# Attention with sinks, then a mixture of attention experts: eight rings of work buffers become two shared pools, with a new instruction list

## The chip, the core and the metric

The kernel runs on one core of one Trainium2 chip. The metric is the device time of one execution in microseconds (us); before the change it is 373.31 us, the median of 3 runs (372.42 to 373.54). A core has a matrix engine (PE, with its weight loads PEld), a vector engine (DVE), a scalar engine (ACT), a general engine (POOL) and a sync engine (SP) that issues the transfers. Each works through its own list of instructions in order and waits for the others through semaphores.

## What is computed

For 4 batches, 8 heads, 768 positions and a head size of 64, the first stage is attention in which each position sees the first 4 positions (the sinks) and the 128 latest ones. Its output, 768 x 512 for each batch, goes through 4 expert attentions, causal and with full rows, each with its own projections; each position keeps 2 of the 4 by a gate.

```python
scores = scale * np.matmul(q, k.transpose(0, 1, 3, 2))
keep = is_sink | in_window
a = softmax(np.where(keep, scores, -1e9))
x = np.matmul(a, v)                      # per head, heads side by side
logits = x @ w_gate                      # top 2 of 4 experts, softmax weights w
for e in range(4):
    q, k, v = x @ wq[e], x @ wk[e], x @ wv[e]
    a = softmax(causal(scale * q @ k.T))
    out += w_e * (a @ v @ wo[e])         # where e is among the two
```

## The kernel before

The work is cut into units: for each batch 4 units of two heads of the first stage (`first`, banded rows) and 2 units of two experts of the second (`second`, wide rows of 1 to 6 blocks of 128 keys). A row of 128 queries goes through the same chain everywhere. PE makes the scores (L664 and L677 for the band, L669 for wide rows) into PSUM banks `b`; DVE masks them, takes the minimum and writes the probabilities' buffer `p` or, for 5 or 6 blocks, `pw` (L919, L955, L842); ACT takes the exponential there with its sum (L924, L959, L854); DVE makes the factor (L718, L719); POOL, or ACT, scales (L933, L980, L864, L862); PE transposes 64 x 64 pieces (L730) into two banks; ACT and DVE copy these to the transposed buffer `pt` (L551, L553, L780); PE multiplies with the values (L703, L707 for the sinks). ACT and DVE split a finished batch chunk `x` into two parts (L534, L539), and the projections (L1055 for queries and keys, L1082 for values) follow, and at the end of a batch the output product (L1131), whose rows go out through a buffer `o`.

The matmuls use the array in four shapes, which the profile writes as rows*columns: 128*128 (projections and output), 64*128 (scores and transposes), 128*64 (products with the values) and 64*64 (L677, an alternative form of a band's score step with 4 matmuls of 196 columns in place of 2 of 260).

The order of all work is a list, `ORDER`, written out in the program: one number for each step, with a letter that puts a step on ACT (a), DVE (v) or POOL (p) or takes the 64*64 form (q). The steps are emitted in that order. The buffer that a step writes is chosen at that moment by `slot`: of the ring with the step's tag the one that a table of costs says comes free first. The real waits are the semaphores that follow from it. While the planned time is under 130 us, `fill_in` puts matmuls on a zero tile (`nought`, L365 to L369) into gaps of the plan on PE. They compute nothing that is used.

```python
best = (None, None)
for n, b in enumerate(self.held[tag]):
    if n in taken:
        continue
    t = 0.0 if b is None else b.free_at(e)
    if t is not None and (best[0] is None or t < best[0]):
        best = (t, n)
return best
```

Before the change each kind of data has a ring of its own: 3 buffers for loaded q (`qn`), 2 for k (`kn`), 3 for v (`vn`), 2 for turned k (`kx`), 12 `p`, 4 `pw`, 4 `pt`, 2 for the differences of v (`dv`) and 2 output rows (`o`).

Of the kernel before, what the change touches and what calls it, by code (L numbers as in the profile page):

```python
# [39 lines left out]
0 44 39 45 46 47 49 1 56 34 42 40 58v 50a 48 51a 57v 52 53v 54a 64 65 67 43 41 37 55 75 76 59 61a 38 60v 66 86q 78 2 87 90 79  # L40
63 114 88 91 77 80 92 81 143 93 97 121q 122 35 98 94 142 68 3 125 95 99 115 69 89 116 123 238 126 96 118 124 70 100 117 119
101 127 239 82 120 83a 148 149v 150v 155 156v 157a 144 71 145 151 84v 72a 73a 128 152 146v 147a 160 153v 171 154v 161 4 163
189 172 162 164 173 102 174 193 182 210q 175 183 186 184 241 187 194 185 190 211 191 243a 242a 217 103 176 244 221 214 218
212 188 195 335 192 129 130 219 245a 5 222 177 246a 251 104a 165 215 247 6 105 220 166 108 252a 267 268 270 253a 256 216 106a
109a 269 430 196 248 131 249a 250a 159 271 107a 257 334 213 259 133 136 25 36 258 134a 197 278q 279 285q 62 158 282 280 283
281 306 289 74 307 286 308 287 223 290 224 111 132a 135a 284 198 313q 291 310 431 137v 311 260 312 225 272 288 314 226 340
199 273 201 433 110 317 200a 292 293 315 203a 138 205a 202a 318 341v 204 261 342a 85 139 112 337 343 316 140 338a 167 113
339a 168a 254 436 319 141 309 344 363 347 169a 240 320 346a 374q 364 366 345a 349a 227 375 378 348a 381q 32 262 26 376 228a
379 229 28 178 294 380 231a 321 33 385 179a 233a 382 230a 386 180a 365 383 384 170 207 30 518 434 232 387 322 29 263 295 402q
234 264v 265v 352 206 377 297 300 296a 403 301a 353 355 404 406 388 298a 181 235 274 299a 407 437 409 208 323 367 275a 209  # L50
276a 356 410 368 411 324a 27 354 435 490 413 255 336 405 408 266 494 303 412 414 325 277 491 31 415 389 350 326a 328 327a 357
451 329a 302 390 492 495 416 236 452 369 358 417 454 418 391 304 237 392v 370 371a 395a 372a 393 330 331 397a 359 394a 360a
351 361a 419 16 21 17 305 396 462q 420v 23 22 423v 453 421 422a 469q 463 473 519 464 19 362 373 399 424 332 466 467 470 425a
522 18 398 440 1086 400 524 465 455 496 24 20 426 427 523 855 401 658 659 441 443 525 428 521 550q 429 471 474 456 468 475
551 557q 552 553 497q 498 499 438 554 660 646 501 472 476 661 444 457 477 442 561 7 562 558 559 555 662 333 478 647 648 560
528 8 9 663 10 502 539 14 15 479 529 531 540 542 766 578q 585q 652 481 11 503 586 563 649 769 480a 12 13 579 767 580 582 587
432 484 583 482a 589 653 532 584 654 655 770 650 651 606 636 543 445 439 446 854 526 590 1092 493 858 530 500 504 505 533 520
534 612 485a 607 618 773 588 857 608 656 541 657 1089 613 637 624 527 619 630 609 631 611 506 625 620 544 632 610a 861 638
614 581 639 633 640a 483v 615 635 626 768 621 627 617 634a 447 556 696 616a 623 641 629 859 642 643 591 592 628a 697 448a 709
507 449a 622a 545 699 458 459a 460a 564 710 711 712 664 665 666 667 508v 509 513a 450 698 644 511v 461 487 514 593 594 700  # L60
510a 512 771 645 670 683 701 668 702 486 669 671 862 724 713 488 672 704p 684 685 703a 686 725 489 535 536a 537a 515 516 546
787 726 517 565 788 727 790 729 547a 728 674 548a 566 687 744 745 791 747 673 746 688 705 748 714 772 567 689 730 675 1175
789 749 569 568v 570v 573v 690p 731 942 750 751 706a 707a 752 572 943 792 948 949 944 950 945 571v 951 952 676 691p 953 538
549 595 946 860 947 574 677a 1087 775 776 678p 777 596a 599v 679 575 680a 597 681a 732 682 779 598a 708 600 576 601a 715 717p
716p 692 718 780 577 693a 719a 778 602 694v 798q 805q 793 753 720v 802 799 826q 806 809 603 721 800 810 827 828 733 807 755a
604 605 803 695 734p 864 829 781 830 875 831 808 804 865 866 833q 867 754p 876 921q 914q 811 735p 878 1090 837 868 915 722
918 916 919 877 834 723 879 954 955 956 801 838 812 835 869 1422 1093 832 925 920 922 917 926 960 839 923 813 957 961 962 958
814 963 959 836 964 736 965 737a 738a 880 870 840 924 760 761a 762a 992 993 994 756 757a 758a 1005 815 740 739 1006 1007 816a
741a 817 820 821v 841 759 742a 1008 782 1176 783 819v 842 784v 818a 927 979 1091 980 785a 843 856 995 928 774 881 893q 886q
981 897 743 887 890 1009 888 996 844a 894 847a 929 863 786 823 889 891 892 898 895 899 845 763 849v 848 871 846a 872v 930 896  # L70
794 873a 900 822 795a 1020 796a 901 902 1010 997 966 967 968 998 982 850 983 764 797 1021 824 851 882 1022 883a 765 825 884a
903 905 909a 906a 931 933 932v 970 1146q 874 908 852 999p 984 934a 1011 1012p 904a 907a 936 853 1013p 985 935v 885 969 1147
# [242 lines left out]
def kernel(  # L315
# [14 lines left out]
    nc = tc.nc  # L330
# [912 lines left out]
```

## Time and profile before

| | |
|---|---|
| median of 3 runs | 373.31 us |
| the profiled execution | 374.27 us, of which the span from the first to the last instruction is 372.2 us |
| PE busy | 364.9 us, 98% of the span |
| PEld, DVE, ACT, POOL busy | 85%, 82%, 76%, 55% |
| granted PE clock | 1.00 of 2.4 GHz |
| moved by DMA | 28.42 MB, mean 76 GB/s |

Busy time is what the records of an engine cover. Records of one engine can overlap: the next instruction starts before the one before it has ended. So the pace of a kind of work is read from one start to the next, and a matmul's own duration is longer than its share. The ends of matmuls are modelled, so a busy PE can still stand for some tens of nanoseconds between two matmuls.

### The profile page before, as it was taken

The page shows a single profiled execution, that of the slowest core. Times are in us where ns is not written, and L with a number is a line of the kernel's source. Part 1 is how long each engine was busy: PE and PEld are TensorE (multiplying, and loading weights), DVE is VectorE, ACT ScalarE, POOL GpSimd, SP SyncE. Part 2 cuts the span into 40 slices and gives each one's busy share as a digit, 9 for nine tenths or more (in the row PEclk, how much of TensorE's full clock was granted, in tenths as well). Part 3 has the DMA queues.
Part 4 walks back from the last instruction along what each step waited for, and adds up shares of the span by engine and source line. Part 5 has one row for each costly group of instructions (what it writes and reads, how often), then busy time and mean ns, then how long its engine had stood idle before and what let it go on. Part 6 is the DMA issues. An engine that isn't in the chain of part 4 may idle for free.

```text
span 372.2 us, 12873 instructions
## 1 busy us (share of the span) xinstructions
PE 364.9 (98%) x4588; PEld 315.7 (85%) x4588; DVE 305.6 (82%) x1415; ACT 284.2 (76%) x984; POOL 203.6 (55%) x395
## 2 busy tenths in 40 slices
PE   8999999999999999999999999999999999999995
PEld 7667878998888888988798889978889889988884
DVE  5899999899999988889989798797879748277851
ACT  3899987798899886468878797589877783539841
POOL 6699966769477184182945185374546260066510
PEclk9999999999999999999999999999999999999999
DMA  8999689900453073046407042013000000011113
GB/s 188 207 168 190 139 148 171 169 4 3 89 104 68 2 145 85 1 136 100 96 4 130 1 71 60 31 59 101 30 4 3 2 2 3 0 53 64 58 53 118
DMA packets 124175, 28.42 MB, mean 76 GB/s; under 512 B 120592, under 2 KB 120848, under 8 KB 124112
## 3 DMA queue, kind: packets, MB, share of 16 engines
q1 hardware_dynamic: 123568, 27.48, 35.6%
q8 instruction: 36, 0.59, 0.7%
q14 instruction: 27, 0.22, 0.2%
q10 hardware_dynamic: 544, 0.13, 0.2%
HBM read 21.05 MB, written 6.29 MB: 73 GB/s over the span
## 4 chain that ended last, share of the span: by engine, by line
PE 88%; DVE 3%; POOL 3%; DMA 2%; issue 2%; ACT 1%; SPq 0%; ACTq 0%; POOLq 0%; DVEq 0%
PE b L703 19%; PE b L1055 18%; PE b L730 11%; PE b L1082 10%; PE b L669 9%; PE b L1131 9%; PE b L664 5%; PE b L677 5%; POOL pw L864 2%; PE b L707 1%; PE b L369 1%; DMA qn<-in_q_dram 1%; POOL p L864 1%; DMA v<-in_moe_wk_dram 1%; ACT p L854 1%
## 5 line engine op out<-in xcount | busy, mean ns | idle before, releaser
L551 ACT ACTIVATE pt<-b 128x256 f32<-128x256 f32 (+3 forms) x186 | 66.8, 407 | 12.7 <-PE b L730 10.3
L959 ACT ACTIVATE p<-p,st 128x132 f32<-128x132 f32 x128 | 51.2, 406 | 6.3 <-DVE st L955 6.1
L933 POOL TENSOR_TENSOR p<-p,st 128x520 f32<-128x520 f32 (+1 forms) x32 | 26.7, 833 | 31.8 <-DVE st L719 22.7
L669 PE MATMUL b<-ks,qs 64*128 64x384 f32 (+3 forms) x384 | 42.1, 339 | 0.0
L703 PE MATMUL b<-pt,v 128*64 128x128 f32 x672 | 41.5, 275 | 0.0
L730 PE MATMUL b<-ident,p 64*128 64x64 f32 x768 | 40.4, 228 | 0.0
L730 PEld LDWEIGHTS b<-ident,p 64*128 64x128 f32 x768 | 33.8, 139 | 6.1 <-issue 1.9
L703 PEld LDWEIGHTS b<-pt,v 128*64 128x64 f32 x672 | 36.5, 137 | 2.5 <-issue 0.7
L703 PE MATMUL b<-pt,vn 128*64 128x128 f32 x448 | 38.0, 279 | 0.0
L1082 PE MATMUL b<-wvh,x 128*128 128x260 f32 x192 | 37.6, 285 | 0.0
L854 ACT ACTIVATE p<-p,st 128x384 f32<-128x384 f32 (+3 forms) x64 | 35.7, 560 | 2.1 <-DVE st L842 1.9
L952 DVE COPY_PREDICATED b<-earlier,b 128x128 f32<-128x128 int32 x128 | 33.6, 288 | 2.8 <-PE b L677 2.3
L955 DVE CUSTOM_DVE_ANT_0 p<-b,pair_mask 128x132 f32<-128x132 f32 x128 | 34.1, 289 | 1.1
L1131 PE MATMUL b<-woh,y 128*128 128x512 f32 (+1 forms) x100 | 34.8, 392 | 0.0
L669 PEld LDWEIGHTS b<-ks,qs 64*128 64x128 f32 x384 | 31.4, 186 | 2.6 <-issue 0.9
L980 POOL TENSOR_TENSOR p<-p,st 128x512 f32<-128x512 f32 x32 | 33.2, 1040 | 0.0
L1055 PE MATMUL b<-x,wqh 128*128 128x512 f32 (+1 forms) x128 | 33.2, 345 | 0.0
L722 POOL TENSOR_TENSOR st<-st,gate 128x2 f32<-128x2 f32 x48 | 9.1, 195 | 44.0 <-DVE st L719 39.5
L1055 PE MATMUL b<-x,wkh 128*128 128x512 f32 (+1 forms) x128 | 33.0, 343 | 0.0
L854 ACT ACTIVATE pw<-pw,st 128x640 f32<-128x640 f32 (+1 forms) x32 | 28.1, 879 | 5.6 <-DVE st L842 5.6
L1082 PEld LDWEIGHTS b<-wvh,x 128*128 128x128 f32 x192 | 30.7, 188 | 0.7
L864 POOL TENSOR_TENSOR pw<-pw,st 128x640 f32<-128x640 f32 (+1 forms) x23 | 30.8, 1356 | 0.9
(137 smaller groups left out, 1049.5 us busy)
## 6 DMA issues: line engine op xcount, KB each, us to landing
vn<-in_v_dram SPq DMA_DIRECT2D x32, 192.0 KB, 3.7
out_dram<-o SPq DMA_DIRECT2D x23, 256.0 KB, 2.0
qn<-in_q_dram SPq DMA_DIRECT2D x48, 96.0 KB, 2.6
kn<-in_k_dram SPq DMA_DIRECT2D x48, 96.0 KB, 2.7
kn<-in_k_dram SPq DMA_DIRECT2D x6, 192.0 KB, 3.6
qn<-in_q_dram SPq DMA_DIRECT2D x6, 192.0 KB, 4.8
o<-in_moe_wo_dram SPq DMA_DIRECT2D x2, 256.0 KB, 3.3
v<-in_moe_wk_dram SPq DMA_DIRECT2D x4, 128.0 KB, 3.1
```

Of the source, the lines that this page charges most:

```text
L551: nc.scalar.activation(dst(), src(), AF.Copy)
L669: nc.tensor.matmul(o, self.qs.t[hs, a, qs], self.ks.t[hs, b, ks], start=n == 0, stop=n == 2)
L703: nc.tensor.matmul(o[e * 64:e * 64 + 64], lhs, rhs, start=e not in self.begun, stop=last and self.done == len(self.steps))
L730: nc.tensor.transpose(t[g].t[:, n, :], x[gs], ident[gs, gs])
L854: nc.scalar.activation(x, x, AF.Exp, bias=st.t[:, 0, es], scale=-1.0, accum_out=st.t[:, 1, es])
L864: nc.gpsimd.tensor_mul(x, x, st.t[:, 2, e:e + 1].to_broadcast([128, n * 128]))
L952: nc.vector.copy_predicated(s2[e].t[:, :128], earlier.bitcast(I32), s2[e].t[:, SW:RW])
L955: nc.vector.tensor_tensor_reduce(out=p.t[:, n, :], in0=s2[e].t[:, :SW], in1=pair_mask, scale=-scale, scalar=BIG, op0=OP.add, op1=OP.min, a ...
L959: nc.scalar.activation(p.t[:, n, :], p.t[:, n, :], AF.Exp, bias=st.t[:, 0, n:n + 1], scale=-1.0, accum_out=st.t[:, 1, n:n + 1])
L1055: nc.tensor.matmul(t.t, w[a][:, c, es], X[b, c].t[:, x, cs], start=c == 0 and m == 0, stop=c == NCH - 1 and m == 2)
L1082: nc.tensor.matmul(t.t[:, :VW], X[b, c].t[:, a, qs], W["wv"][w][:, c, :], start=c == 0 and n == 0, stop=c == NCH - 1 and n == 2)
L1131: nc.tensor.matmul(t.t[:, a0:z0], Y[b, c].t[:, a, qs], W["wo"][w][:, c, a0:z0], start=c == 0 and n == 0, stop=c == EP - 1 and n == 2)
```

## The change

The eight rings `qn`, `kn`, `vn`, `kx`, `pw`, `pt`, `dv`, `o` and the ring `p` become two pools: 15 buffers `n` of 792 columns and 22 buffers `p` of 528. A loaded q, k or v, a turned k, a row of 5 or 6 blocks and a transposed piece of 6 sub-blocks take any free `n`; other probabilities, shorter transposed pieces, differences, the loaded output weights and the output rows take any free `p`. A band's transposed piece, formerly one `pt` of 8 sub-blocks, is now two `p` of 4. A wide row with 4 blocks has its transposes in two parts of 2 blocks, which adds 32 steps (2707 to 2739). One mask is stored in 128 columns less its unused part. The list `ORDER` is new in full, also its letters. Of the list one line of each stands for the rest.

```diff
-0 44 39 45 46 47 49 1 56 34 42 40 58v 50a 48 51a 57v 52 53v 54a 64 65 67 43 41 37 55 75 76 59 61a 38 60v 66 86q 78 2 87 90 79
...
+44 39 45 0 46 1 49 50a 51a 52 54v 53v 64 65 56 47 34 48 40 2 143 59 55 75 57a 67 58v 61v 60a 37 86 35 76 68 114 38 78 41 66
...
@@ -348,10 +349,10 @@
-    kinds = {"qn": (3, 768, F32), "kn": (2, 768, F32), "vn": (3, 768, F32), "qs": (1, 2 * S, F32R), "ks": (1, 2 * NB * SW, F32R),
-             "x": (6, 2 * S, F32R), "kx": (2, NB * SW, F32), "v2": (1, 1536, F32), "y0": (1, 2 * S, F32R), "y1": (1, 2 * S, F32R), "p": (12, 4 * SW, F32), "pw": (4, 768, F32),
-             "dv": (2, 512, F32), "pt": (4, 1024, F32), "psk": (4, 128, F32), "sk": (2, 128, F32R), "vs": (2, 4 * D, F32R),
-             "o": (2, 512, F32), "gate": (2, 4 * NB * E, F32), "gates": (1, 2 * NB * E * E, F32), "st": (6, 20, F32),
+    kinds = {"n": (15, NB * SW, F32), "p": (22, 4 * SW, F32), "qs": (1, 2 * S, F32R), "ks": (1, 2 * NB * SW, F32R),
+             "x": (6, 2 * S, F32R), "v2": (1, 1536, F32), "y0": (1, 2 * S, F32R), "y1": (1, 2 * S, F32R),
+             "psk": (4, 128, F32), "sk": (2, 128, F32R), "vs": (2, 4 * D, F32R),
+             "gate": (2, 4 * NB * E, F32), "gates": (1, 2 * NB * E * E, F32), "st": (6, 20, F32),
              "b": (8, 512, F32)}
@@ -415,12 +416,12 @@
         for i, ns in ((0, n_sink), (1, n_sink)):
-            m = consts.tile([128, RW], F32, name=f"bmask{i}")
+            m = consts.tile([128, RW if i else 128], F32, name=f"bmask{i}")
             nc.vector.memset(m, 0.0)
             if i:
                 nc.vector.memset(m[:, 128:SW], masked)
                 window_mask(m[:, :128], 128, ns)
-            window_mask(m[:, SW:], 0, 0 if i else ns)
+            window_mask(m[:, SW:] if i else m, 0, 0 if i else ns)
             row_mask[i] = m
@@ -479,7 +480,7 @@
         for c0 in range(0, cols, whole):
-            st = buf(tag, NB * E * D if tag == "v2" else n)
+            st = buf(tag, NB * E * D) if tag == "v2" else buf("p", n)
@@ -563,7 +564,7 @@
             self.nk = hi - self.k0
-            self.qs, self.ks = (None, buf("kx", 1, NB * SW)) if exact else (buf("qs", 2, S), buf("ks", 2, NB * SW))
+            self.qs, self.ks = (None, buf("n", 1, NB * SW)) if exact else (buf("qs", 2, S), buf("ks", 2, NB * SW))
@@ -740,7 +741,7 @@
         t, n = two(8, 64), 2 * len(cols)
-        pt = buf("pt", n, 128)
+        pt = buf("p" if n <= 4 else "n", n, 128)
@@ -764,7 +765,7 @@
-        t, pt, sk = two(8, 64), buf("pt", 8, 128), buf("sk", 128)
+        t, pts, sk = two(8, 64), [buf("p", 4, 128) for _ in range(2)], buf("sk", 128)
         psk, kept, vs, made_vs = sinks
@@ -772,18 +773,18 @@
         tt = plan.step(prio, {PE: 313}, tr, normed + kept, t, [p, psk], mode="ROWS")
-        moved, moved_sk = [], []
+        moved, plain, moved_sk = [], [], []
         for g in range(2):
             gs = slice(64 * g, 64 * g + 64)
             def tri(g=g, gs=gs):
-                nc.vector.tensor_mul(pt.t[:, 4:, gs], t[g].t[:, :4, :], own[:, None, gs].to_broadcast([128, 4, 64]))
+                nc.vector.tensor_mul(pts[1].t[:, :, gs], t[g].t[:, :4, :], own[:, None, gs].to_broadcast([128, 4, 64]))
             new, used, behind = once(moved_sk, sk)
             moved_sk.append(evacuate(prio, lambda gs=gs: sk.t[:64, gs], lambda g=g: t[g].t[:64, 4, :], 64, [tt], [t[g], *used], new, behind=behind))
-            new, used, behind = once(moved, pt)
+            new, used, behind = once(moved, pts[1])
             moved.append(plan.step(prio, {DVE: 65 + 1.04 * 256}, tri, [tt], new, [t[g], *used], behind=behind))
-            new, used, behind = once(moved, pt)
-            moved.append(evacuate(prio, lambda gs=gs: pt.t[:, :4, gs], lambda g=g: t[g].t[:, :4, :], 256, [tt], [t[g], *used], new, behind=behind))
+            new, used, behind = once(plain, pts[0])
+            plain.append(evacuate(prio, lambda gs=gs: pts[0].t[:, :, gs], lambda g=g: t[g].t[:, :4, :], 256, [tt], [t[g], *used], new, behind=behind))
@@ -798,10 +799,10 @@
                     for e in range(2):
-                        acc.add(i + r, e, diff[0](i + r, e) if c else value[0](i + r - 1, e), pt.t[:, 4 * c + 2 * r + e, :], r == 1 and c == 1)
+                        acc.add(i + r, e, diff[0](i + r, e) if c else value[0](i + r - 1, e), pts[c].t[:, 2 * r + e, :], r == 1 and c == 1)
         new, used = acc.bufs()
-        acc.steps.append(plan.step(prio + AV_LAG, {PE: 872}, av, moved + value[1](None) + diff[1], new,
-                                   [pt] + value[2] + diff[2] + used, fifo="av", mode="cols"))
+        acc.steps.append(plan.step(prio + AV_LAG, {PE: 872}, av, moved + plain + value[1](None) + diff[1], new,
+                                   pts + value[2] + diff[2] + used, fifo="av", mode="cols"))
@@ -816,7 +817,7 @@
             else:
-                ps, sums = [buf("pw" if n * 128 > 4 * SW else "p", n * 128) for _ in range(2)], []
+                ps, sums = [buf("n" if n * 128 > 4 * SW else "p", n * 128) for _ in range(2)], []
             one = lambda e, ps=ps, n=n: ps[e].t[:, e, :] if n <= 2 else ps[e].t
@@ -863,7 +864,7 @@
                 norms[e] = plan.step(prio - WIDE_N, {POOL: pool_cost(128 * n), ACT: 190 + 0.833 * 128 * n}, norm, [r], (), [ps[e], st])
-            for c0, c1 in parts:
+            for c0, c1 in [(0, 2), (2, 4)] if n == 4 else parts:
                 transposed(prio, acc, i, list(dict.fromkeys(ps)), cols[c0:c1],
@@ -880,7 +881,7 @@
-            dv = buf("dv", NB - 2, 2, D)
+            dv = buf("p", NB - 2, 2, D)
             d0, v0 = max(first, 2), 0
@@ -916,7 +917,7 @@
             def low(e=e):
-                nc.vector.tensor_tensor_reduce(out=p.t[:, e, a:], in0=s2[e].t[:, a:RW], in1=row_mask[i][:, a:], scale=-scale,
+                nc.vector.tensor_tensor_reduce(out=p.t[:, e, a:], in0=s2[e].t[:, a:RW], in1=row_mask[i], scale=-scale,
                                                scalar=BIG, op0=OP.add, op1=OP.min, accum_out=st.t[:, 0, e:e + 1])
@@ -1006,7 +1007,7 @@
         for which, (tag, src) in enumerate((("qn", q), ("kn", k), ("vn", v))):
-            t = buf(tag, NB, 2, D)
+            t = buf("n", NB, 2, D)
             nat.append(t)
@@ -1122,7 +1123,7 @@
     def store(b, i, prio):
-        qs, t, o, last = slice(i * 128, i * 128 + 128), buf("b", Dm), buf("o", Dm), None
+        qs, t, o, last = slice(i * 128, i * 128 + 128), buf("b", Dm), buf("p", Dm), None
         halves = cut("0 256 512") if (b, i) == (B - 1, NB - 1) else [(0, Dm)]
         for a0, z0 in halves:
             for c in range(EP):
```

What the new list does to the order of the instructions is seen at three places. The first is SP's list soon after the start, from the loads of the sinks' values (`v_0`) on; `qn`, `kn`, `vn` or now `n` receive q, k and v. Before:

```order
L512 DMA v_0_81<-in_v_dram 4x16x64 x4
L1019 DMA kn_67<-in_k_dram 128x6x64 x2
L1019 DMA qn_64<-in_q_dram 128x6x64 x2
L517 DMA v_0_81<-v_0_81 16x1024 x3
L1019 DMA qn_65<-in_q_dram 128x6x64 x2
L1019 DMA kn_66<-in_k_dram 128x6x64 x2
L1019 DMA vn_69<-in_v_dram 128x6x64 x2
L1019 DMA kn_67<-in_k_dram 128x6x64 x2
L526 DMA vp<-v_0_81 16x1024
L1023 DMA qn_63<-in_q_dram 32x24x32 x4
```

and now:

```order
L513 DMA v_0_108<-in_v_dram 4x16x64 x4
L1020 DMA n_67<-in_k_dram 128x6x64 x2
L1020 DMA n_68<-in_q_dram 128x6x64 x2
L518 DMA v_0_108<-v_0_108 16x1024 x3
L1020 DMA n_69<-in_k_dram 128x6x64 x2
L1020 DMA n_71<-in_q_dram 128x6x64 x2
L1020 DMA n_72<-in_q_dram 128x6x64 x2
L527 DMA vp<-v_0_108 16x1024
L1020 DMA n_74<-in_k_dram 128x6x64 x2
L1024 DMA n_76<-in_k_dram 32x24x32 x4
```

The second load of v (`vn_69`) is gone from these rows, since it stands later, and q and k of further units come before it, each into a buffer that nothing has used so far. The second place is ACT's list up to the copy of the fourth chunk `x` of the first batch (a 128x512 write of `x`), with which the first stage of that batch ends but for its last third. Before:

```order
L492 ACTIVATE wqh<-v_0_81 128x260 x2
L492 ACTIVATE wqh<-v_0_81 128x244
L924 ACTIVATE p_88,st_123<-p_88,st_123 128x260
L551 ACTIVATE pt_102<-b_129 128x4x64
L492 ACTIVATE wqh<-v_0_81 128x260
L534 ACTIVATE x_75<-b_128 128x256
L551 ACTIVATE pt_102<-b_132 128x4x64
L534 ACTIVATE x_76<-b_130 128x512
```

and now:

```order
L552 ACTIVATE sk_115<-b_132 64x64
L493 ACTIVATE wqh<-v_0_108 128x244
L493 ACTIVATE wqh<-v_0_108 128x260
L552 ACTIVATE p_81<-b_132 128x4x64
L535 ACTIVATE x_104<-b_131 128x256
L925 ACTIVATE p_80,st_127<-p_80,st_127 128x128
L493 ACTIVATE wqh<-v_0_108 128x260
L535 ACTIVATE x_105<-b_134 128x512
```

The copy is ACT's row 116 of the list before and 123 of the new one, counted from 0. The third place is PE's list at the end of the program, where the last products with the values (`v_0`) and the output products (`woh`, `wol`) stand. Before, between the last transposes and the last output products:

```order
L1131 MATMUL b_131<-woh,y_0_83 128x512
L1131 MATMUL b_131<-wol,y_0_83 128x512
L1131 MATMUL b_131<-woh,y_0_83 128x512
L703 MATMUL b_125<-pt_105,v_0_81 64x128 x6
L703 MATMUL b_125<-pt_103,v_0_81 64x128 x6
L703 MATMUL b_125<-pt_102,v_0_81 64x128 x4
L1131 MATMUL b_129<-woh,y_0_82 128x512
L1131 MATMUL b_129<-wol,y_0_82 128x512
L1131 MATMUL b_129<-woh,y_0_82 128x512
L1131 MATMUL b_129<-woh,y_0_83 128x512
L1131 MATMUL b_129<-wol,y_0_83 128x512
L1131 MATMUL b_129<-woh,y_0_83 128x512
```

and now:

```order
L731 MATMUL b_133<-ident,n_68 128x64
L704 MATMUL b_132<-p_81,v_0_108 64x128 x2
L704 MATMUL b_132<-p_99,v_0_108 64x128 x4
L704 MATMUL b_132<-p_79,v_0_108 64x128 x4
L704 MATMUL b_130<-n_65,v_0_108 64x128 x6
L704 MATMUL b_132<-n_75,v_0_108 64x128 x6
L704 MATMUL b_132<-p_88,v_0_108 64x128 x4
L704 MATMUL b_130<-n_73,v_0_108 64x128 x6
L704 MATMUL b_130<-p_82,v_0_108 64x128 x4
L704 MATMUL b_130<-n_63,v_0_108 64x128 x6
L1132 MATMUL b_128<-woh,y_0_109 128x512
```

Before, 12 output matmuls stand ahead of the last 16 products with values. Now 42 such products stand behind 64 transposes in one piece, and all output products that are left, 42 matmuls, follow.

## Rows read from the trace of the kernel before

**Rows 1.** Busy us (instructions) of each engine by stretch, then clock, DMA share, GB/s.

```profile
core 0: us, PE busy (x) PEld busy (x) DVE busy (x) ACT busy (x) POOL busy (x), PEclk, DMA share, GB/s
...
20.00:40.00 20.00, 18.67 (x284) 14.43 (x282) 19.45 (x115) 19.98 (x96) 19.18 (x36) 1.00 0.90 170
...
60.00:340.00 280.00, 279.91 (x3487) 247.42 (x3481) 234.23 (x1063) 216.65 (x728) 147.85 (x284) 1.00 0.27 56
340.00:360.00 20.00, 19.92 (x312) 17.73 (x309) 14.95 (x51) 16.23 (x42) 8.04 (x13) 1.00 0.10 38
```

**Rows 2.** Waits of PE: line waited for, us in total, times, longest; last of four.

```profile
PE b L664 <- ACT qn L551: 0.5, 1, 0.5
```

**Rows 3.** ACT in order of time, 0 to 53 us: start us, us, instruction.

```profile
11.19 0.51 ACT L924 ACTIVATE p<-p,st 128x260 f32<-128x260 f32 x1
...
11.70 0.50 ACT L924 ACTIVATE p<-p,st 128x260 f32<-128x260 f32 x1
...
13.62 0.39 ACT L959 ACTIVATE p<-p,st 128x132 f32<-128x132 f32 x1
...
14.01 0.39 ACT L959 ACTIVATE p<-p,st 128x132 f32<-128x132 f32 x1
...
47.27 0.45 ACT L551 ACTIVATE pt<-b 128x128 f32<-128x128 f32 x2 [0.28 <-PE b L730]
```

**Rows 4.** PE in order of time, 40 to 60 us: start us, us, instruction.

```profile
44.74 0.26 PE L730 MATMUL b<-ident,psk 64*128 64x64 f32 x1
44.80 0.27 PE L707 MATMUL b<-sk,vs 64*128 64x128 f32 x1
...
47.42 0.89 PE L677 MATMUL b<-kx,qn 64*64 64x196 f32 x16
48.24 1.09 PE L703 MATMUL b<-pt,vn 128*64 128x128 f32 x16
...
51.22 0.39 PE L703 MATMUL b<-pt,vn 128*64 128x128 f32 x4
51.44 0.39 PE L703 MATMUL b<-pt,dv 128*64 128x128 f32 x4
51.76 0.73 PE L1055 MATMUL b<-x,wkh 128*128 128x512 f32 x2
...
53.35 1.23 PE L677 MATMUL b<-kx,qn 64*64 64x196 f32 x24
54.50 0.73 PE L1055 MATMUL b<-x,wkh 128*128 128x512 f32 x2
```

**Rows 5.** The chain that ended last, in order of time: start us, us, what.

```profile
13.00 2.12 PE b L369 x12
...
27.34 2.88 DMA v<-in_moe_wk_dram
...
95.73 0.86 PE b L664 x8
```

**Rows 6.** All engines in order of time, the end: start us, us, instruction.

```profile
351.66 1.25 POOL L864 TENSOR_TENSOR pw<-pw,st 128x640 f32<-128x640 f32 x1
...
356.48 1.21 PE L730 MATMUL b<-ident,pw 64*128 64x64 f32 x32
...
356.97 1.25 ACT L551 ACTIVATE pt<-b 128x256 f32<-128x256 f32 x3 [0.44 <-PE b L730]
357.18 1.57 DVE L553 COPY pt<-b 128x256 f32<-128x256 f32 x3
...
365.61 0.72 ACT L551 ACTIVATE o<-b 128x256 f32<-128x256 f32 x3 [2.60 <-PE b L1131]
...
367.97 0.40 PE L1131 MATMUL b<-woh,y 128*128 128x512 f32 x1
368.45 0.60 ACT L551 ACTIVATE o<-b 128x512 f32<-128x512 f32 x1 [2.12 <-PE b L1131]
```

**Rows 7.** Transfers out: issues, KB each, median us from issue to landing.

```profile
out_dram<-o SPq DMA_DIRECT2D x23, 256.0 KB, 2.0
...
out_dram<-o SPq DMA_DIRECT2D x2, 128.0 KB, 1.7
```

More of the change, by code (lines that the diff above doesn't have):

```diff
@@ L44 @@
[L44 to L48, printed above, removed]
@@ new lines @@
+1029 1030 1004a 988 970 971 854 989 934 875 876a 990p 972 801 828 855 856 877v 886 829 857 887a 888a 907 909 1182 908a 912
+910a 911a 1048 1049 1031 935 1032 913a 938a 974 1033 936v 939a 937 1035 878 1050 889 940 991p 1034 915 1104 1115 1051 1105
+1107 941a 1154 973 1116 1118 914 916 942 1036 1052 1018 1019a 1155 1053 1158 1117 1020a 1156 1159 1055 943 944 1133q 1054
+1037 917 1161q 1126q 1162 1163 1096 945 1038p 975 1130 976 1322 1039a 1310 1056 1187 1134 1189 1127 1188 1106 1165 1528 1435
+1128 1135 1160 1164 1185 1166 1323 1131 1311 1324 978a 977a 1119 1108 1325 1137 1057 1326 1327 1058a 1059p 1312 1313 1314
@@ new lines @@
+1093 1800 2189 1793 1803 1949 1950 1804 1724 2187 1822 1823 1708 1805 1659 1806 2100 1689 1707 1725a 1726a 1690 1691 1709a
+2107 1710a 1727 1772 1952 1731 1784 1711 2190 2193 1951 1953 2015 1936 1937 1828 1824 1938 1968 1807 1810a 1969 2102 1813v
+1770 1846 1870 1732 1733 1773 1970 1940 1809 1812 1785 1847 1831 1954 2013 1939 1808v 1941 2104 1774 1852 1811v 1871 1853
+1872 1858 1848 1876 1864 1859 1877 1854 1878 2191 1873 1832 1849 1851 1860 1833 1834 1855 1850v 1874v 1865 1857 1861 1862a
+1879 1875 1856v 1881 1866 1867 1863 1869 1880a 1775 1971 1910 1776a 2103 1777a 1882 1972 1973 1868a 1974 1911 1923 1912 1913
@@ new lines @@
+1756a 2054 2072 2051 2055 1744a 2045 1753 2130q 2077q 2075 2052 2131 2132 2081 2158q 2134 2123 1998a 2133 2078 2137q 2286
+2135 1738 2048 2287 2138 2139 2141 2136 2159 2140 1739 2142 2036 2124 2162 2288 2289 2037 2143 2144 2082 2083 1746 1747 1919
+2125 2056 2160 2290 2291 2057 2163 1958 1740a 2079 1748a 1920v 1921a 2145 1959a 1960v 2058 1945 2108 1073 2109 1745 1946a
+2111 1947a 2207 2059 2208 1980 2027 2061 2112 2080 2062a 2028v 2029a 1981a 1982a 1999p 2210 2060v 2064 1922 1948 1962 2065v
+1932 1963a 2004 1933a 2005a 2019 2209 2110 1964v 2165q 2063v 1934v 2166 2225q 2169 2170 2218q 2006a 2222 2219 2220 2226 2227
@@ new lines @@
+2501 2512 2544 2545 2547 2548 2528 2546 2586 2422 2587 2440 2423 2513 2514 2428 2515 2434 2549 1737 2503 2502 2441 2504 2550
+2568 2446 2442 2452 2447 2453 2598 2443 2424 2551 2429 2425 2427 2454 2435 2455 2448 2426v 2449 2450v 2436 2516 2430 2571
+2418 2437 2431 2457 2489 2451 2599 2570 2419 2600 2530 2439 2445 2432a 2433 2458 2588 2601 2459 2592 2589 2438v 2444v 2604
+2460 2461 2593 2531 2420a 2505 2506p 2605 2594 2456a 2490 2491 2572 2421 2532a 2552 2410 2590 2591 2602 2603 2553 2554p 2492
+2573 2595 2411 2596 2597 2493p 2606 2494a 2495 2412v 2610 2533a 2649 2611 2496a 2668 2612 2650 2574p 2651 2497a 2555p 2636
@@ L145 @@
+2619 2417 2658 2620a 2621a 2647v 2409 2678p 2585 2659v 2660a 2700 2662 2704 2701a 2663v 2702a 2705a 2680 2684 2622 2661 2706v
+2635 2664v 2681a 2682a 2683 2648 2685v 2665 2686a 2707 2687 2666 2703 2708 2667 2714 2722 2715 2716a 2718 2709 2730 2710 2723
+2719 2711 2720a 2717 2721 2712a 2713 2724v 2731 2725 2726 2727 2732v 2733 2728a 2729 2734 2735 2736a 2737a 2738
 """
```

181 lines of the change are left out of this document (82 added, 99 removed).

## Prediction

> **What bounds the kernel now.** I read the busy times by stretch first. From 60 to 340 us PE is busy for 279.91 of 280 us at a granted clock of 1.00, and from 340 to 360 us for 19.92 of 20 [rows 1]. Next the waits of PE: another engine or a transfer is named for only four, all at the start, the last of them 0.5 us [rows 2]. So from about 50 us on the time is the sum of what PE issues: the matmuls, and what is lost where the array changes its shape. Before that it is different. From 20 to 40 us PE shows 18.67 us, part of it matmuls on zeros, while ACT shows 19.98, DVE 19.45 and POOL 19.18 [rows 1]: that is a stage of exponentials and copies, with little for PE to do. In ACT's order of time the next gap after 20.6 us is at 47.27 us, and it is 0.28 us long [rows 3]. The first projection starts at 51.76 us [rows 4]. I take ACT as the bound of this first stage, and PE as that of the rest.
>
> I make the sum against the profiled execution, 374.27 us (its span of 372.2 and 2.07 around it). It is 0.96 us above the median of 373.31, so at the end I apply the difference to the median.
>
> **The change, part by part.** The pools as such add no instruction to a load, an exponential or a product: a buffer is chosen when the program is built. What they cost or give lies in the waits and in the new list, which I count.
>
> *First stage.* I count ACT's list up to the copy of the fourth chunk `x`. Before there are 8 exponentials of 128 columns, 9 of 260, 32 of 132 and 13 copies of 64 columns for the sinks ahead of it; now 10, 8, 33 and 15. Everything else that ACT does there has the same number. From start to start an exponential of 132 with its sum takes 0.39 us (13.62 to 14.01), one of 260 takes 0.51 (11.19 to 11.70) [rows 3]. I give 128 columns the 0.39 of 132, and a copy of 64 columns 0.1, an estimate well below the 0.39. That is 3 x 0.39 - 0.51 + 2 x 0.1 = **+0.9 us** until the projections can start. From below, the gaps that ACT has before 13 us could shrink with loads that come earlier, and the term is 0. From above, the list itself holds more filler: 2390 columns of zeros before, 2931 now. At 2.12 us for the 1117 columns (512, 512 and 93) at 13.00 us [rows 5] the 541 more are 1.0 us; if this came on top, the term would be +1.9. I take +0.9, since ACT's queue is the one without gaps.
>
> *Changes of shape.* Scores and transposes share the shape 64*128, and run into each other: a transpose starts at 44.74, a product with the sinks' values, 64*128 too, at 44.80 [rows 4]. I count no loss there. Every other change costs. Sixteen 64*64 matmuls take from 47.42 to 48.24 us until the next kind starts, 24 take from 53.35 to 54.50: the eight more cost 0.33, so 16 cost 0.66 and the change 0.16. Four products with values take 0.22 (51.22 to 51.44), but the projection after the next four starts 0.32 after them: 0.10 [rows 4]. I take 0.15, nearer to the first, because a projection's first matmuls are slowed as well. In PE's list I count 161 such changes before and 139 now. 37 and 32 of them stand ahead of the first projection, where ACT is the bound and they are worth nothing. Behind it there are 124 and 107. 17 x 0.15 = **-2.55 us**; with 0.10 it is -1.7, with 0.2, as an upper estimate, -3.4.
>
> *Score steps.* The new list does more of the bands' scores before the first projection and gives two more steps the 64*64 form. Behind the first projection PE has 38 matmuls of 260 columns for 36, and 140 of 64*64 for 152. One of 260 is two records of 0.1075 (eight in 0.86 us [rows 5]), one of 64*64 two of 0.041 (24 less 16 in 0.33 [rows 4]): +0.43 - 0.98 = **-0.55 us**. The other matmuls are the same in number and size.
>
> *End.* The last PE instruction ends at 368.37 us; then ACT copies 512 columns, 368.45 to 369.05 [rows 6], and the row of 256 KB lands. In the new list the last to be copied are the last 256 columns, in two copies of 128. A group of one copy of 256 and two of 128 took 0.72 us [rows 6]; the two alone I estimate at 0.45. The transfer is of 128 KB, which lands in 1.7 us where 256 KB takes 2.0 [rows 7]. 0.15 + 0.3 = **-0.45 us**. If the larger store just ahead of it on SP lands last, the term is -0.1.
>
> *What costs nothing.* The split of the transposes of rows with 4 blocks makes 16 more copies of at most 0.4 us on ACT and DVE, some 3 us each over the kernel; from 60 to 340 us ACT has 63 us free and DVE 46 [rows 1]. The two `p` in place of one `pt` add no instruction. Loads after 60 us have the DMA queues nearly free (share 0.27 [rows 1]), and no PE wait on a load is shown there, so earlier loads gain nothing there.
>
> The sum is 0.9 - 2.55 - 0.55 - 0.45 = **-2.65 us**: 371.6 for the profiled execution, and 370.7 for the median. All ends together run from -0.0 - 3.4 - 0.55 - 0.45 = -4.4 to +1.9 - 1.7 - 0.55 - 0.1 = -0.45.
>
> **The rivals.** *The start gains from earlier loads.* The transfer of the first projection's weights lies on the chain that ended last, 2.88 us at 27.34 [rows 5]. If free buffers let it go that much earlier, the start gains at most this instead of losing 0.9: 370.7 - 0.9 - 2.9 = 366.9. For it: SP's loads of k and q before it wait for readers of the three or two buffers. Against: it stands behind the copy of the sinks' values, as before, and ACT has no gap for it to fill. The Trainium skill, "DMA: Bandwidth & Descriptors", section "Rules for kernel authors", says that a transfer should be issued early and waited for late, which speaks for this rival; no row after the start shows PE waiting on a load.
>
> *The last transposes wait for their copies.* The new list puts 64 transposes in one piece near the end, where it had 48 and 32 with other work behind. After the 32 of 356.48 us, which take 1.21, the copies go on until 358.75 us on both engines [rows 6], hidden under output matmuls. For 64 the copies need about twice the 1.78 us from 356.97 on, so they end 4.05 us after the first transpose, 1.65 after the last one; the products that follow use the early pieces first. At most 1.65 us: 372.35, no difference that counts. The Trainium skill, "TensorEngine Tiling (Array Packing)", section "PSUM Bottleneck", says that tiling speeds up PE but not the copies out of PSUM, which can become the bottleneck; that would be this case. The trace agrees in so far as the copies outlast the transposes.
>
> *The changes of shape cost nothing in sum.* If the stops only hide waits that come anyway, the -2.55 falls away: 373.2, the same. Against it: the loss stands at each change that I looked at, also where nothing is waited for.
>
> *The last normalizations come late, and it is slower.* POOL scales a row of 640 columns in 1.25 us [rows 6], and with no output matmuls left between the last wide rows PE has nothing to cover one that is late. If four of these rows each stand one such step later, PE waits 5 us: 375.7. It decides from 2.65 us, thus three of them. Against: from the last scores to the last transpose the old list has 84 transposes and 48 products with values on PE, the new one 124 and 42. At 0.038 for a transpose (1.21 for 32 [rows 6]) and 0.11 for a product of two records (four records in 0.22 [rows 4]) that is 8.5 and 9.3 us: the last rows have more time than before.
>
> **How the numbers follow.** Chances: the forecast 0.52, earlier start 0.12, waiting for copies 0.14, changes worth nothing 0.10, late normalizations 0.12. A measurement of this kernel tells about 0.3% from no change, 1.1 us, so faster is below 372.2 and slower above 374.4. The forecast and the early start lie below, which gives 0.64 for faster; the two middle cases 0.24; slower 0.12. The forecast's own range is 368.9 to 372.9, from the ends of its terms. For 8 in 10 I go from 368.0, since the early start can't often be had in full, to 374.0, which takes in the two middle cases.
>
> **What would show it.** Right: the first projection starts at 52 to 53 us; PE again without gaps behind it; the time from there to the end of PE shorter by about 3 us; the span some 2.6 us shorter, and a last copy of 128 columns. Wrong: PE waits with a name behind 60 us, on copies or POOL above all; or the first projection at 54 us or later; or before 50 us, for the early start. If PE is full and the span is the same, the price of a change of shape was wrong.

## The result, and the profile after

The new kernel takes 369.99 us (median of 5 runs, 368.71 to 371.25) against 373.54 of the kernel before beside it: a ratio of 0.991, 95% interval 0.9881 to 0.9939, thus faster by 2.3 to 4.4 us. The forecast was 370.7, in a range of 368.0 to 374.0. A second set of runs of the same kernel gave 369.57 us and 0.9901 (0.9881 to 0.9921). The profiled execution took 370.37 us with a span of 368.4, against 374.27 and 372.2: 3.8 us less in the span, where the sum had 2.65.

First the head of the page after, and its chain that ended last.

```profile
span 368.4 us, 12893 instructions
...
PE 361.4 (98%) x4588; PEld 313.9 (85%) x4588; DVE 305.6 (83%) x1422; ACT 282.8 (77%) x988; POOL 205.6 (56%) x400
...
PE 86%; DMA 5%; SPq 5%; POOL 1%; issue 1%; ACT 1%; DVE 0%; ACTq 0%; DVEq 0%
```

Next the busy us by stretch after, columns as in [rows 1].

```profile
20.00:40.00 20.00, 18.98 (x270) 13.56 (x268) 18.77 (x111) 19.10 (x91) 18.64 (x37) 1.00 1.01 172
...
60.00:340.00 280.00, 279.80 (x3479) 249.01 (x3477) 238.93 (x1088) 217.68 (x737) 154.19 (x293) 1.00 0.29 55
340.00:360.00 20.00, 20.00 (x362) 18.62 (x359) 11.70 (x37) 14.03 (x35) 5.95 (x9) 1.00 0.16 59
```

And the waits of PE after, all that have a name; the last is the only one behind 56 us.

```profile
PE b L1149 <- DVE lanes L414: 1.1, 1, 1.1
PE b L731 <- DMA n<-in_q_dram: 0.7, 1, 0.7
PE b L731 <- DVE st L956: 0.4, 1, 0.4
PE b L665 <- DVE n L554: 0.2, 1, 0.2
PE b L665 <- ACT p L552: 0.2, 1, 0.2
PE b L1083 <- POOL wvl L497: 0.2, 1, 0.2
```

From 60 us on PE is as full as in [rows 1], so the time that the new kernel saves was saved in what PE issues, or at the start. The balance of the start has changed: from 20 to 40 us ACT now has 0.90 us free where it had 0.02, and loads and SP's queue make up 10% of the chain, where they had 2%.

PE in order of time at the first projection, then all engines at the end:

```profile
50.67 1.23 PE L678 MATMUL b<-n,n 64*64 64x196 f32 x24
51.83 0.74 PE L1056 MATMUL b<-x,wqh 128*128 128x512 f32 x2
```

```profile
364.24 1.13 ACT L552 ACTIVATE p<-b 128x512 f32<-128x512 f32 x3 [1.14 <-PE b L1132]
...
364.62 0.28 PE L1132 MATMUL b<-woh,y 128*128 128x256 f32 x1
```

The projections start at 51.83 us (51.76 before [rows 4]). PE ends at 364.90 (368.37 [rows 6]), the span 3.50 later (3.83). So in this pair of traces the three stages gave +0.07, -3.54 and -0.33 us, where the prediction had +0.9, -3.10 and -0.45.

The +0.07 can't be taken to a tenth. Two kernels below, `own_shape` and `same_shape`, are the new one unchanged until 70 us. Their first projections, in that order:

```profile
50.95 0.73 PE L1061 MATMUL b<-x,wqh 128*128 128x512 f32 x2
```

```profile
50.69 0.73 PE L1062 MATMUL b<-x,wqh 128*128 128x512 f32 x2
```

So the same start ends between 50.69 and 51.83 us, 1.1 us apart, from one execution to the next. With the old list there are two traces, at 51.76 and 51.06 (`pools_old_list`). The first stage thus gave something between -1.1 and +0.8 us.

To part the work from the changes of shape I gave every kind of matmul (line and columns) one price and every ordered pair of shapes another, and fitted them by least squares to the starts of PE's records in eight traces: these two and six of the kernels below. What no price explains is called idle. The table is a reckoning and no view of the profile.

| us | to the first projection, before | after | behind it, before | after |
|---|---|---|---|---|
| matmuls, those on zeros too | 38.44 | 38.79 | 296.41 | 296.01 |
| changes of shape | 7.10 | 6.06 | 18.74 | 15.86 |
| idle | 5.10 | 5.86 | 1.07 | 0.92 |

Fitted in other ways to the same records (long gaps left out or weighed less, the first 15 us left out, other traces beside these two), the changes of shape save 2.6 to 2.8 us behind the first projection, where the table has 2.88, and 0.6 to 0.7 ahead of it, where the table has 1.04. How the rest is split between matmuls and idle moves by some us with the way of fitting, so the single entries of those two rows show little.

### The profile page after: what moved, and what is told of

Its sections match the earlier page's. It is cut to its first block, busy times and chain, and to the rows that moved or that the text cites. A ratio compares the mean times of both kernels' runs of the same rounds, so it can differ in the third digit from the quotient of the medians.

```text
span 368.4 us, 12893 instructions
## 1 busy us (share of the span) xinstructions
PE 361.4 (98%) x4588; PEld 313.9 (85%) x4588; DVE 305.6 (83%) x1422; ACT 282.8 (77%) x988; POOL 205.6 (56%) x400
## 4 chain that ended last, share of the span: by engine, by line
PE 86%; DMA 5%; SPq 5%; POOL 1%; issue 1%; ACT 1%; DVE 0%; ACTq 0%; DVEq 0%
PE b L704 21%; PE b L1056 17%; PE b L731 11%; PE b L1083 10%; PE b L1132 9%; PE b L670 9%; PE b L678 4%; PE b L665 4%; DMA n<-in_q_dram 2%; SPq L1020 2%; PE b L708 1%; DMA v<-in_moe_w_gate_dram 1%; DMA v<-in_moe_wk_dram 1%; SPq L487 1%; SPq L1024 1%
## 5 line engine op out<-in xcount | busy, mean ns | idle before, releaser
L552 ACT ACTIVATE p<-b 128x256 f32<-128x256 f32 (+2 forms) x162 | 55.9, 380 | 20.2 <-PE b L731 10.1
L855 ACT ACTIVATE p<-p,st 128x512 f32<-128x512 f32 (+3 forms) x64 | 35.5, 555 | 12.0 <-DVE st L843 11.9
L731 PE MATMUL b<-ident,p 64*128 64x64 f32 x768 | 43.3, 229 | 0.2
L670 PE MATMUL b<-ks,qs 64*128 64x384 f32 (+3 forms) x384 | 40.3, 335 | 0.0
L704 PE MATMUL b<-p,n 128*64 128x128 f32 x448 | 38.1, 278 | 0.1
L554 DVE COPY p<-b 128x256 f32<-128x256 f32 (+2 forms) x72 | 28.8, 415 | 6.8 <-PE b L1132 4.9
L1056 PE MATMUL b<-x,wkh 128*128 128x256 f32 (+1 forms) x128 | 32.8, 339 | 0.0
L865 POOL TENSOR_TENSOR n<-n,st 128x768 f32<-128x768 f32 (+1 forms) x24 | 32.4, 1363 | 0.7
L865 POOL TENSOR_TENSOR p<-p,st 128x256 f32<-128x256 f32 (+3 forms) x43 | 29.8, 710 | 1.2
L925 ACT ACTIVATE p<-p,st 128x128 f32<-128x128 f32 (+1 forms) x64 | 29.2, 458 | 1.3 <-DVE st L920 0.8
```

The lines of the kernel that those rows point to most:

```text
L552: nc.scalar.activation(dst(), src(), AF.Copy)
L670: nc.tensor.matmul(o, self.qs.t[hs, a, qs], self.ks.t[hs, b, ks], start=n == 0, stop=n == 2)
L704: nc.tensor.matmul(o[e * 64:e * 64 + 64], lhs, rhs, start=e not in self.begun, stop=last and self.done == len(self.steps))
L731: nc.tensor.transpose(t[g].t[:, n, :], x[gs], ident[gs, gs])
L855: nc.scalar.activation(x, x, AF.Exp, bias=st.t[:, 0, es], scale=-1.0, accum_out=st.t[:, 1, es])
L865: nc.gpsimd.tensor_mul(x, x, st.t[:, 2, e:e + 1].to_broadcast([128, n * 128]))
```

## Experiments

Each kernel is the new one with the edit shown, except the first, which is the old one. "Against the new kernel" compares ratios to the kernel before, 0.991 being that of the new one, times 373.5 us.

**The pools alone.** The old list and its steps, with shared buffers:

```diff
-    kinds = {"qn": (3, 768, F32), "kn": (2, 768, F32), "vn": (3, 768, F32), ...
+    kinds = {"n": (14, NB * SW, F32), "p": (15, 4 * SW, F32), ... "pt": (4, 1024, F32), ...
```

> The old list of steps with pools: 14 buffers n for q, k, v, their turned copies and the wide rows, 15 buffers p for the rest, the four wide buffers pt kept. My theory: the gain comes from the new list (fewer changes of the array's shape), the pools by themselves give nothing, so 373.5 us, within 1.1 us of before, with 161 changes of shape. Rival, the pools let the start's loads go earlier and that is the gain: the first projection 1 to 3 us before 51.8 us, and 370.5 to 372.5 us.

Measured: 373.5 us, ratio 0.9991 (0.9979 to 1.0002). Of its trace, PE at the first projection, then the longest wait of SP's queue in the first 52 us, here and in the kernel before (line waited for: us in total, times, longest):

```profile
51.06 0.74 PE L1055 MATMUL b<-x,wkh 128*128 128x512 f32 x2
```

```profile
SPq L486 <- POOL psk L975: 1.5, 1, 1.5
```

```profile
SPq L486 <- POOL psk L975: 4.4, 1, 4.4
```

The first projection comes 0.70 us earlier than before, no more than two executions of one start can differ, and SP waits 2.9 us less ahead of the weights. The time shows nothing of it. So the pools are worth nothing that can be told by themselves. The gain came with the list. Counted along the new list, it holds 15 `n` and 22 `p` at once, exactly what the pools have, up to 11 loads of q, k and v among them, where the rings had 8; the list can't run on the rings.

**The price of a change of shape.** 48 pairs of matmuls on zeros, once behind products of the same shape (`same_shape`, two pairs at each of 24 places), once between two projections (`own_shape`, one at each of 48):

```diff
+ if own and was == "cols" and s.mode in ("ROWS", "rows", "quad"): fill("cols", own, 128); fill("cols", own, 128)
```

```diff
+ if own and was == "FULL" and s.mode == "FULL": fill("cols", own, 128)
```

> The new kernel with 48 pairs of matmuls on zeros (64 columns of the array, 128 moving columns each) behind its 70th us, put where the array already has that shape, so that no change of shape is added. Each matmul on zeros costs about 0.055 us by the products with values (four in 0.22), thus 48 x 0.11 = 5.3 us: 375.3 against 370.0.

> The same 48 pairs, but each between two projections of the full array, so that 96 changes of shape are added. By the price of the prediction, 0.15 us for each, 14.4 us more than with the pairs in their own shape: 389.7. With 0.10 it is 384.9, with 0.20 394.5. Rival, changes cost nothing in sum: 375.3, as with the pairs in their own shape.

Measured: 379.73 us and 397.59 us on one chip, ratios 1.0170 (1.0147 to 1.0192) and 1.0649 (1.0633 to 1.0666). The difference of 0.0479, 17.9 us, over 96 changes is **0.186 us for each**; the two intervals leave 0.176 to 0.197. The rival, nothing in sum, is out for this pair of shapes, 128*128 and 128*64, there and back. Of the 22 changes by which the new list has fewer, 5 are of this pair and 15 between 64*128 and 128*64, in either direction. The price of those no experiment took: for them there is only the fit. The pairs themselves cost 9.7 us against the new kernel and not 5.3: a matmul here is two records, and I had counted one. PE in `own_shape`, a pair between projections and a stretch without one:

```profile
121.77 0.40 PE L1061 MATMUL b<-x,wkl 128*128 128x512 f32 x1
122.09 0.44 PE L373 MATMUL b<-nought 128*64 128x128 f32 x4
122.46 0.72 PE L1061 MATMUL b<-x,wqh 128*128 128x512 f32 x2
123.03 0.40 PE L1061 MATMUL b<-x,wql 128*128 128x512 f32 x1
123.26 0.63 PE L1061 MATMUL b<-x,wkh 128*128 128x512 f32 x2
123.73 0.39 PE L1061 MATMUL b<-x,wkl 128*128 128x512 f32 x1
```

From 121.77 to 123.03 it is 1.26 us, where three such matmuls without the pair take 0.70 (123.03 to 123.73). Of the 0.56 the pair's four records are 0.22, by the products with values in [rows 4]; 0.34 for two changes is 0.17 each. Part of it falls on the matmuls behind the change, which the prediction had put down as "a projection's first matmuls are slowed as well" and priced too low. The Trainium skill, "TensorEngine Tiling (Array Packing)", section "Key Properties", says that a change of tiling mode drains the engine, and gives no price; the trace agrees in so far as each change here costs PE 0.17 to 0.19 us.

**More work on PE at the start.** Ten pairs of matmuls on zeros, of 512 columns, without a change of shape, in two windows:

```diff
+ if own and kept and lo < t < hi and extra < 10: fill(kept, own, 512)   # late 36.4 to 49.5 us, early 18 to 32.5, of the plan's time
```

> The new kernel with ten more pairs of matmuls on zeros (512 moving columns, without a change of shape) on PE in the 14 us ahead of the first projection: 10 x 0.45 = 4.5 us of PE. If PE is already the bound from about 38 us on, the first projection and the end come 4.5 us later: 374.5. If ACT bounds the stage up to the first projection, as the prediction has it, most of the pairs fall into PE's gaps, and it is at most 1 us: 371.

> The same ten pairs between the 18th and the 33rd us. PE has gaps and fillers there (before 36 us about 4.6 us without work that is explained, of it 3.5 us behind 15 us). If the loads and ACT bound that stage, at most 2 us of the 4.5 come through: 370 to 372. If PE bounds there too: 374.5.

Measured: 378.41 us, ratio 1.0141 (1.0115 to 1.0167), and 376.65 us, 1.0100 (1.0065 to 1.0136): 8.6 and 7.1 us against the new kernel, both with some 1.5 us of uncertainty. Again the pairs were twice as long as I had expected, four records of 0.22 us, 8.9 us in all. So within the uncertainty all of the late work comes through, and four fifths of the early. PE in `pe_late` at its first projection:

```profile
61.25 0.72 PE L1062 MATMUL b<-x,wqh 128*128 128x512 f32 x2
```

That is 9.4 us later than in the new kernel, more than the pairs, since this trace also had the slow beginning that the last set of runs is about. The prediction's view, that matmuls ahead of the first projection cost nothing because ACT bounds until there, is wrong: of the 8.9 us of late work at most 1.8 can have been hidden. Whether a saving of 1 us comes through in full is not shown by it.

**More work on ACT at the start.** 30 copies of 100 columns into a spare buffer, in the same two windows:

```diff
+ if e == ACT and lo < t < hi and extra < 10: for _ in range(3): nc.scalar.activation(spare, nought[:, :100], AF.Copy)
```

> The new kernel with 30 more copies of 100 columns on ACT (0.13 us each from start to start, 4.0 us together) in the 14 us ahead of the first projection. By the prediction (ACT bounds until then): 4.0 us later, 374.0. If PE bounds from 38 us on, with copies that stand some steps ahead: 0 to 1.5 us, 370 to 371.5.

> The same 30 copies on ACT between the 18th and the 33rd us. If ACT bounds that stage: 4.0 us later, 374.0. If the loads bound it (ACT has 0.9 us free from 30 to 40 us): about 1 us less than 4.0, 373.

Measured: 377.3 us, ratio 1.0118 (1.0088 to 1.0148), and 380.24 us, 1.0181 (1.0146 to 1.0216): 7.8 and 10.1 us against the new kernel. The copies were longer too. ACT in `act_late`, then PE's two longest waits, and a window of ACT with the granted clock (the last three numbers: clock, DMA share, GB/s):

```profile
38.84 0.91 ACT L378 ACTIVATE spare<-nought 128x100 f32<-128x100 f32 x3
```

```profile
PE b L675 <- ACT p L562: 2.6, 1, 2.6
PE b L741 <- ACT p L562: 1.4, 3, 0.7
```

```profile
44.00:48.00 4.00, 3.81 (x16) 0.50 0.95 138
```

Three copies take 0.91 us, so the 30 are 9.1. Of these 7.8 come through, and not all of it need be ACT's own time: PE waits for ACT, 2.6 us at a stretch until 42.4 us, and from 44 to 48 us the granted clock is 0.50 (1.2 GHz). So ACT counts in this stage, as the prediction has it, and so does PE: before the first projection the two wait for each other by turns, and neither has room for 4 us more.

**Lighter loads.** q and k behind the first batch read in long rows:

```diff
- x.rearrange("(n r) (h c) -> h r n c", r=32, c=32)[h, :, 4 * a:4 * z, :]
+ x.rearrange("(h r n) (m c) -> h r (n m) c", h=2, r=32, c=32)[h]
```

> The new kernel with the loads of q and k for the batches behind the first read in rows of 3 KB where they were read in pieces of 128 bytes. The bytes and the number of transfers are the same; the elements come in another order, so the blocks of 32 that the transposes on DVE rely on are left out. If the DMA engines bound the start (busy share 0.97 until 51.8 us, 1.09 from 30 to 40), the first projection comes 1 to 3 us earlier, and the time is 367 to 369. If ACT or PE bounds it, nothing changes: 370, with a DMA share well below 0.97.

Measured: 368.61 us, ratio 0.989 (0.9872 to 0.9907). The window to 52 us of this kernel, of the new one (PE busy, clock, DMA share, GB/s), and PE at the first projection of this one:

```profile
0.00:52.00 52.00, 48.80 (x683) 1.00 0.83 185
```

```profile
0.00:52.00 52.00, 48.67 (x679) 1.00 0.97 175
```

```profile
50.89 0.74 PE L1056 MATMUL b<-x,wqh 128*128 128x512 f32 x2
```

The DMA engines are freed as expected, 0.83 for 0.97. The first projection, at 50.89 us, lies among those of the new kernel's start (51.83, 51.48 in its second trace, and 50.95 and 50.69 above). The ratio lies 0.1 to 0.2% below those of the new kernel, inside the intervals. So neither the trace nor the time can tell what the loads cost the start from nothing.

**Two loads exchanged.**

```diff
- ... 226th step of the list: 144 (v) ... 241st: 430 (q) ...
+ ... 226th step of the list: 430 (q) ... 241st: 144 (v) ...
```

> The new kernel with two loads in the other order: q of the first unit of the second batch (issued at 28.9 us, landed at 35.8, and on the chain that ended last) ahead of the v issued at 27.4 us. If the landing of that q holds the start, it gains up to 1.4 us: 368.6 to 369.5. If not: 370.0.

Measured: 371.9 us, ratio 0.997 (0.9955 to 0.9985): slower than the new kernel by about 2.2 us, against both expectations. The exchange brought in what I had not thought of, PE in order of time:

```profile
44.57 0.69 PE L370 MATMUL b<-nought 64*128 64x512 f32 x1
44.79 1.19 PE L370 MATMUL b<-nought 64*128 64x512 f32 x6
45.82 0.28 PE L370 MATMUL b<-nought 64*128 64x136 f32 x1
```

The plan fills the gaps that it reckons PE to have with matmuls on zeros. With the other order it reckons with gaps here that the chip doesn't have: some 1.3 us of zeros at 44.57, and 0.3 more behind, where PE is full; the new kernel has none between 36 and 54 us. What the landing of that q is worth stays open, since the fillers hide it, and so does the slow beginning of this trace, which comes next.

**The start once more.** In the trace of `q_first` what follows 5.3 us came later than in that of the new kernel, with the same instructions up to there. PE in order of time, the new kernel first, then `q_first`, then the kernel before:

```profile
5.38 0.97 PE L370 MATMUL b<-nought 64*128 64x432 f32 x4
6.27 0.34 PE L731 MATMUL b<-ident,n 64*128 64x64 f32 x4
```

```profile
5.54 1.78 PE L370 MATMUL b<-nought 64*128 64x432 f32 x4
7.09 0.45 PE L731 MATMUL b<-ident,n 64*128 64x64 f32 x4
```

```profile
5.59 1.06 PE L369 MATMUL b<-nought 64*128 64x214 f32 x4
6.42 0.67 PE L730 MATMUL b<-ident,qn 64*128 64x64 f32 x8
```

Four records of 432 columns take 0.89 us until the next kind starts, or 1.55: 1.9 or 1.1 columns per ns, which I read as the two levels of 2.4 and 1.2 GHz; in the kernel before it is 1.0. That is read from the durations alone, for the column of the granted clock shows 1.00 in all three. So I ran the new kernel again, and two with fewer of these zeros:

```diff
- (0.3 if since < COLD else 0.6)
+ (0.1 if since < COLD else 0.6)     # thin_fill; no_cold_fill has 0.0
```

> The new kernel once more, unchanged, beside the next two. In its first trace a pair of matmuls on zeros of 432 columns at 5.4 us took 0.97 us, in that of the kernel with the two loads exchanged, the same up to there, 1.78: the array's clock had risen in the one and not yet in the other, and what followed came 1.2 us later. If that is so for single executions, its times lie in two groups about 1.2 us apart, around 369 and 370.5 us, with a median of 369.5 to 371.3.

> The new kernel with the fillers of the first 8 us cut to a third (432 to 144 columns, 241 to 80). They stand ahead of the transposes of the first k and cost 1.5 us at the high clock, 2.9 at the low one. If they only delay these, the executions with the low clock at the start gain up to 1.2 us, and the median is 369.0 to 370.0. If they are what raises the clock, it rises later, and the median is the same or higher, 370 to 371.5.

> The new kernel with none of these fillers. If they only delay: 368.8 to 369.8, with the times closer together. If they raise the clock: the first scores run at the low clock, and it is 370.5 to 372.

Measured: 369.57 us (368.78, 369.22, 369.53, 369.61, 371.04, 371.13), 371.47 and 371.25; ratios 0.9901 (0.9881 to 0.9921), 0.9938 (0.9919 to 0.9957) and 0.9929 (0.9911 to 0.9948). The new kernel's times do fall into two groups some 1.5 us apart here, though not in the first five runs, so two groups are not shown. Fewer zeros are not better; both medians are higher by 1.7 to 1.9 us. Windows of `thin_fill` (five engines, clock, DMA share, GB/s):

```profile
7.00:9.00 2.00, 1.58 (x23) 1.57 (x25) 1.24 (x8) 0.68 (x3) 0.20 (x1) 0.72 1.21 258
9.00:11.00 2.00, 2.00 (x12) 1.93 (x10) 1.03 (x5) 2.00 (x10) 1.54 (x3) 0.50 1.03 219
```

The new kernel shows 1.00 in both stretches. So in this trace PE, with fewer zeros, was busy for 1.58 of the 2 us in which the granted clock began to fall, and the first scores ran at the lower one. But this execution, at 369.98 us, is the fastest of its six, the others taking 370.53 to 372.31. So it is not shown that the fall of the clock makes this kernel's median higher; what does stays open. No version was found that beats the new kernel beyond the intervals.

## Why the prediction was nearly right

*Changes of shape: right in kind, and near in price.* The 0.15 us is 0.186 by experiment, for one pair of shapes. By the fit it is 0.16 on the mean of all: 25.84 us for the 161 changes before, 21.92 for the 139 after. The 22 that went were somewhat dearer, 3.92 us or 0.18 each; by the other fits they are 0.15 to 0.16. Behind the first projection the table has -2.88 where I had -2.55, which lies inside my -1.7 to -3.4. That the changes, and not something else in PE's order, made this difference rests on the fit, and on PE being full with the same matmuls but for the score steps: no run took these 22 changes alone.

*First stage: the step that failed.* The prediction counted "37 and 32 of them stand ahead of the first projection, where ACT is the bound and they are worth nothing". Work of PE there does come through (`pe_late`), and the fits price these changes at 0.6 to 1.0 us. That I gave the stage one bound, from ACT having the smallest gaps, was the error: from 20 to 40 us PE had 18.67 of 20 busy [rows 1], DVE and POOL over 19, and stages so full have little cover to give. Nor did the copy of the fourth chunk, up to which I had counted ACT's list, come later. Before, then after:

```profile
50.39 0.60 ACT L534 ACTIVATE x<-b 128x512 fp32r<-128x512 f32 x1
```

```profile
49.86 0.59 ACT L535 ACTIVATE x<-b 128x512 fp32r<-128x512 f32 x1
```

It starts 0.53 us earlier, with the longer list ahead of it. The projection follows 1.37 us behind it before and 1.97 after; PE has other work in between. So the +0.9 is not seen in these traces, and the first projection came at 51.83 us where I had said 52 to 53. Part of this may be luck: both traces of the old list began slowly (856 columns of zeros in 0.83 and 0.82 us), and the four of the new list's unchanged start began at the faster rate. Of the new list with a slow beginning there are only kernels with another change; in the one without the first zeros, `no_cold_fill`, whose first four transposes take 0.48 us (0.34 in the new kernel's trace), the first projection starts at 52.94 us. With equal beginnings the +0.9 may be right; that is not shown.

*Score steps:* -0.40 for matmuls behind the first projection by the table, -0.3 to -0.4 by the other fits, -0.55 forecast. *End:* -0.33 for -0.45. The last copies did end earlier behind PE (365.37 less 364.90 is 0.47, where it was 0.68 [rows 6]). But the store of 128 KB landed in 2.0 us where I had 1.7 from [rows 7]:

```profile
out_dram<-p SPq DMA_DIRECT2D x2, 128.0 KB, 2.0
```

*What costs nothing* held: from 60 to 340 us PE shows 279.80 of 280 busy with 16 more copies on ACT and DVE.

*The rivals.* The earlier start is out as a cause: with pools SP waits less for buffers, but `pools_old_list` gains nothing, and lighter loads gain nothing that can be told. The waiting for copies and the late normalizations are out: behind 56 us the one wait of PE that has a name is 0.2 us, on the low part of the values' weights. The changes that are worth nothing in sum are out by `own_shape`. Of the signs named for "right", PE without gaps and the last copy of 128 columns came as said, the 3 us from the first projection to PE's end were 3.54, and the 52 to 53 us for the first projection were 51.83.

Put together by the table, the changes of shape are -3.92 us, matmuls -0.05, idle +0.61, and what lies between the start of PE's last matmul and the end of the span -0.47: -3.8 us, the difference of the spans. The terms add up because idle is what is left over; that the changes are by far the largest is the fit's finding, and the experiment's price for one pair bears it out.

## What to carry to other kernels

A cost that an engine pays per instruction or per change counts in every stretch in which that engine has no real idle time, also where another engine is fuller; call a stage covered only after work added to the covered engine has been seen to vanish. The price of such an event is best had from the same instructions put at two kinds of place, one with the event and one without. Shared buffers gave nothing by themselves here; they allowed an order that the separate rings can't hold, and the gain of that order has to lie in something that can be counted, here 22 changes of the array's shape. And one trace is not enough to read a stage to a tenth of a us: four traces of the same first 50 us lay 1.1 us apart.

## What the runs showed beyond that

The start differs from execution to execution: the same 432 columns of zeros, behind the same instructions, took 0.89 us in the new kernel's trace and 1.55 in that of `q_first`, while the column of the granted clock shows 1.00 in both. The Trainium skill, "TensorE: Matmul & The Clock Gate", Part 1, says that the number of matmuls at the low clock at a kernel's start varies from run to run; the traces agree, if these durations are the two levels of the clock. With ACT delayed early the clock fell and stayed low for long; windows of `act_early` (five engines, clock, DMA share, GB/s):

```profile
22.00:24.00 2.00, 0.62 (x16) 0.25 (x10) 1.11 (x7) 1.91 (x9) 1.99 (x5) 1.00 0.88 197
24.00:26.00 2.00, 0.80 (x16) 0.61 (x16) 0.00 (x0) 1.87 (x9) 0.00 (x0) 0.58 1.45 176
26.00:28.00 2.00, 0.00 (x0) 0.00 (x0) 1.55 (x9) 1.91 (x9) 1.10 (x4) 0.50 0.94 99
...
32.00:34.00 2.00, 2.00 (x16) 0.81 (x12) 1.38 (x9) 1.89 (x11) 0.00 (x0) 0.50 1.45 157
34.00:36.00 2.00, 2.00 (x24) 1.09 (x21) 1.89 (x13) 1.41 (x7) 0.97 (x4) 0.50 1.43 182
```

PE had been busy for 0.62 of 2 us before the clock fell, was idle from 26 to 28 us, and the clock stayed at 0.50 with PE full from 32 to 36. That may be why 9.1 us of ACT's time cost 10.1; the difference of 1.0 lies inside the uncertainty of 1.7, so it is not shown. And three copies of 100 columns into one and the same buffer took 0.30 us each, where I had worked out 0.13 from copies into different ones; whether it is the common target was not tried.
